# Hash attention and FFN on one core: whole-tile loads in one queue, part of the first batch's hash by column-tiled matmuls and moves, and a new order

## The chip, the core and the metric

The kernel runs on one core of a Trainium2 chip. The core has five engines that each work through their own list of instructions in order: TensorE (PE, the matrix unit; PEld is its loading of weights), VectorE (DVE), ScalarE (ACT), GpSimd (POOL) and SyncE (SP). Sixteen DMA engines move data between device memory (HBM) and the on-chip memory SBUF, or within SBUF; a transfer is started by an instruction on SP, ACT or POOL. Transfers issued by SP are on queue 1 of the trace, those issued by POOL on queue 0. Matmul results go to a second memory, PSUM. Engines wait for one another by semaphores, and a transfer reports its end by a semaphore too.

The metric is the time of one execution on the device in microseconds (us), as the median of several executions. Lower is better.

## The reference

Four batches of eight heads, 768 positions, 64 numbers each. Queries and keys are hashed by the signs of six projections, a query attends only to keys with the same hash, and the result goes through a normalization and a two-layer network (FFN) with a residual. In short:

```python
q_bits = (np.einsum('bhsd,dk->bhsk', q, proj) > 0)        # proj: 64 x 6
k_bits = (np.einsum('bhsd,dk->bhsk', k, proj) > 0)
mask = q_bucket[:, :, :, None] == k_bucket[:, :, None, :]  # bucket: the six bits as a number
scores = np.where(mask, scale * np.matmul(q, k^T), -1e9)
attn = softmax(scores)
x = np.matmul(attn, v)                                     # heads side by side: 768 x 512
xn = (x - mu) / np.sqrt(var + 1e-06) * g_ln
out = x + np.maximum(xn @ w_ch1, 0.0) @ w_ch2              # 512 -> 2048 -> 512
```

## The kernel before

**Tiling.** Work is cut into 12 units of 256 queries: unit u belongs to batch u // 3. The eight heads are two groups g of four, and the 768 keys are three pieces kp of 256. That makes 72 score tiles, numbered s = 6u + 3g + kp. Each tile is a list of small steps, written as words such as `S.t.7.2`: the step's name, the engine's letter (v DVE, a ACT, p POOL, s SP, t PE), and its arguments.

- `S` (function `S_`): scores of one tile by 24 matmuls. The mask is not a select: hash bits are stored in a tile `G` as +0.5 and -0.5, a matmul of the bits of keys and queries is added into the same PSUM as the scaled scores, and only equal hashes come out large enough to survive the exponential. The last argument is 2 for all four heads, or 0 or 1 for a half (the PSUM tiles scA and scB).
- `E`: the exponential on ACT, two instructions per tile, into a tile that has three buffers. `A`: attention times values, 16 matmuls into the PSUM tile `acc`.
- `na`, `nb`, `nc`, `ce`, `rs`: division by the row sum, statistics, and the normalized `xc`. `ft` and `fc` (unit 0 only) or `fl` (a DMA transpose) turn it into `xnT`.
- `F`: 8 matmuls of the first FFN layer; `R`: its relu, on DVE or ACT; `D`: 4 matmuls of the second layer; `Z`: residual; `O`: the store. From unit 1 on, all `F` use the one PSUM tile `f1`, so an `F` can start only when the `R` of the one before has read it.

**Loading and hashing.** Keys and queries come as 768 KB tiles `X` (one per batch, group, and q or k); DVE turns them (`tn` in batch 0, `tu` later) and ACT, DVE or POOL cast them to bf16 (`ca`, `CA`) as `qb` and `kb`. There are four buffers for `X`.

- Batch 0 is loaded in parts, `lx.s.g.t.from.to` (t is 0 for q and 1 for k; the last two are the pieces of 256 positions). Its hash is `ha`, two matmuls of 256 columns in f32 with the padded projection `pfull`, which leaves the bits of all four heads on the partitions where `S` wants them; `bi` on DVE makes them 0.5 or -0.5 and writes `G`. There are twelve `ha` and `bi`, one per group, q or k, and piece.
- Later batches are loaded whole (`LX.s.b.g.t`). Their hash is `hm`: 16 column-tiled matmuls with the small projection `p32`, which put the bits of different positions on different partitions; `bt` makes them 0.5 or -0.5 in a tile `B`, and 16 small transfers per group, `mo`, bring them to their places in `G`.
- v comes as `lv`: two whole transfers of 768 KB for batch 0, and transfers of 192 KB for the others. POOL casts it (`cv`), sets a column of ones (`on`) and sums it (`su`); `sp` on PE and `sc` spread the sum. The weights come as eight transfers issued by POOL, `lw1` and `lw2`, which turn f32 into bf16 on the way.

**What sets the order.** Nothing is scheduled while the kernel is built. The string `ORDER` lists some 1,100 words; the loop at the end reads them one by one, and each engine's instructions follow in that order. What the layer below adds is the waits: for data, for a free buffer, and for the transfers. There are eight completion semaphores for the transfers of SP and ACT, which take them in turn, so that a transfer is issued only when the one eight before it has landed (where no other wait implies it).

The functions `hq`, `bq` and `mq` are in the kernel before too, but no word of its `ORDER` calls them.

Of the kernel before, what the change touches and what calls it, by code (L numbers as in the profile page):

```python
# [17 lines left out]
lp.a mem.v tab.a lx.s.0.0.0.1 warm.t tn.v.0.0.0 pf.v ha.t.0.0.0 lx.s.0.1.1.3 ca.a.0.0.0 tn.v.0.1.2 ha.t.0.1.2  # L18
tn.v.0.1.1 bi.v.0.0.0 ha.t.0.1.1 lx.s.0.1.0.1 tn.v.0.1.0 ca.a.0.1.0 bi.v.0.1.2 ca.p.0.1.2 S.t.2.0 E.a.2.0 S.t.2.1
E.a.2.1 lv.s.1.0.0 on.p.0 on.p.1 lx.s.1.0.0.1 ha.t.0.1.0 bi.v.0.1.1 lw1.p.3 ca.v.0.1.1 S.t.1.0 E.a.1.0 S.t.1.1  # L20
E.a.1.1 tn.v.1.0.0 ca.v.1.0.0 bi.v.0.1.0 ha.t.1.0.0 S.t.0.0 bi.v.1.0.0 E.a.0.0 S.t.0.1 E.a.0.1 pmem.p p32.p
lv.s.0.0.4 cv.p.0.0.0 cv.p.0.0.2 su.p.0.0 lx.s.1.1.0.3 tn.v.1.1.1 ha.t.1.1.1 ca.v.1.1.1 bi.v.1.1.1 A.t.1.1
lv.s.1.0.3 A.t.1.0 lw1.p.0 lv.s.1.0.2 S.t.4.2 E.a.4.1 E.a.4.0 tn.v.1.1.0 ha.t.1.1.0 bi.v.1.1.0 ca.p.1.1.0 A.t.0.1
A.t.2.1 tn.v.1.1.2 ca.p.1.1.2 sp.t.0.0 sc.v.0.0 A.t.0.0 A.t.2.0 na.v.0.0 nb.v.0.0 nc.v.0.0 S.t.3.2 E.a.3.1 E.a.3.0
ha.t.1.1.2 bi.v.1.1.2 S.t.5.2 E.a.5.0 E.a.5.1 lx.s.0.0.1.3 tn.v.0.0.1 ha.t.0.0.1 tn.v.0.0.2 ca.v.0.0.1 lv.s.0.4.4
cv.p.0.4.2 cv.p.0.4.0 A.t.3.2 A.t.4.2 su.p.0.4 sp.t.0.4 lg.s sc.a.0.4 bi.v.0.0.1 S.t.8.2 E.a.8.1 lx.s.1.0.1.3
tn.v.1.0.1 ca.p.1.0.1 tn.v.1.0.2 ca.v.1.0.2 ha.t.1.0.2 ha.t.1.0.1 bi.v.1.0.2 lw1.p.2 LX.s.1.0.0 tu.v.1.0.0.1
tu.v.1.0.0.3 E.a.8.0 S.t.7.2 E.a.7.0 E.a.7.1 A.t.5.2 LX.s.1.0.1 tu.v.1.0.1.3 bi.v.1.0.1 LX.s.1.1.0 ha.t.0.0.2
S.t.6.2 E.a.6.0 E.a.6.1 na.v.0.1 A.t.8.2 A.t.7.2 nb.v.0.1 nc.v.0.1 ce.v.0.0 ce.v.0.1 ft.t.0.1 fc.a.0.1 lw1.p.1
ca.p.0.0.2 bi.v.0.0.2 lv.s.1.4.3 lw2.p.0 ft.t.0.0 S.t.9.2 E.a.9.1 E.a.9.0 lv.s.1.0.1 su.p.1.0 cv.p.1.0.0  # L30
tu.v.1.0.1.1 fc.v.0.0 F.t.0.7 R.v.0.7 F.t.0.6 R.a.0.6 lv.s.1.4.2 LX.s.2.0.0 lw2.p.2 A.t.6.2 na.v.1.0 nb.v.1.0
nc.v.1.0 tu.v.1.0.1.0 S.t.10.2 E.a.10.0 E.a.10.1 lw2.p.1 F.t.0.0 R.v.0.0 A.t.9.2 F.t.0.5 R.a.0.5 S.t.11.2 E.a.11.1
E.a.11.0 rs.p.0 tu.v.1.0.0.2 tu.v.1.0.1.2 CA.p.1.0.1 LX.s.1.1.1 lv.s.1.4.0 A.t.10.2 F.t.0.2 R.v.0.2 lv.s.1.4.1
cv.p.1.4.0 F.t.0.1 R.v.0.1 S.t.14.2 E.a.14.0 E.a.14.1 A.t.11.2 F.t.0.4 R.a.0.4 tu.v.1.0.0.0 F.t.0.3 R.a.0.3 na.v.1.1
nb.v.1.1 nc.v.1.1 ce.v.1.1 fl.s.1.1 ce.v.1.0 fl.s.1.0 A.t.14.2 CA.v.1.0.0 S.t.12.2 E.a.12.1 hm.t.1.0 bt.v.1.0
mo.s.1.0.2.3 tu.v.1.1.0.3 tu.v.1.1.1.3 tu.v.1.1.0.1 tu.v.1.1.0.2 tu.v.1.1.1.1 mo.s.1.0.0.2 mo.s.1.0.0.3 mo.s.1.0.0.0
mo.s.1.0.3.2 mo.s.1.0.3.3 mo.s.1.0.1.1 tu.v.1.1.1.2 D.t.0.0.0 E.a.12.0 S.t.13.2 E.a.13.0 mo.s.1.0.2.2 mo.s.1.0.1.0
tu.v.1.1.0.0 mo.s.1.0.0.1 D.t.0.0.1 D.t.0.0.2 F.t.1.2 R.v.1.2 tu.v.1.1.1.0 E.a.13.1 S.t.16.2 E.a.16.1 E.a.16.0
F.t.1.1 R.v.1.1 A.t.12.2 A.t.13.2 F.t.1.0 R.v.1.0 S.t.15.2 E.a.15.1 mo.s.1.0.2.1 LX.s.2.0.1 F.t.1.5 R.v.1.5
mo.s.1.0.3.0 lw2.p.3 D.t.0.0.3 mo.s.1.0.3.1 E.a.15.0 mo.s.1.0.1.2 hm.t.1.1 S.t.17.2 E.a.17.0 E.a.17.1 mo.s.1.0.1.3  # L40
su.p.1.4 mo.s.1.0.2.0 na.v.2.0 A.t.16.2 nb.v.2.0 A.t.15.2 nc.v.2.0 bt.v.1.1 mo.s.1.1.1.0 mo.s.1.1.0.0 mo.s.1.1.0.3
# [547 lines left out]
```

## Time and profile before

| | |
|---|---|
| median of 3 executions | 312.07 us (311.89 to 312.83) |
| profiled execution | 312.83 us; its span 311.1 us |
| PE busy | 294.3 us, 95% of the span |
| DVE, ACT, POOL busy | 185.7, 181.5, 89.7 us |
| read from HBM, written to it | 27.53 MB, 6.29 MB |
| first score matmul | 10.36 us |
| first FFN matmul | 39.01 us |

The span is what the profile covers; what lies around it is the difference to the execution's time, 1.7 us. Times in the profile count from the start of the span. A line of the order of time reads: start, length, engine, source line, operation, output <- inputs, shape, number of instructions merged, and in brackets how long the engine was idle before and what ended that. PE's records overlap, since matmuls are pipelined and their ends are modelled. "Packet records" are the DMA engines' own list of what they moved and when.

### The profile page before, as it was taken

What the parts mean: (1) busy time and instruction counts of PE and PEld (TensorE: products, weight loads), DVE (VectorE), ACT (ScalarE), POOL (GpSimd) and SP (SyncE); (2) the same over time, 40 slices, a digit from 0 to 9 for tenths busy, and PEclk for the clock granted to TensorE, in tenths of its full rate; (3) what the DMA queues carried; (4) which work ended last, traced back from release to release, by engine and by line L of the source; (5) the groups of instructions that cost most, each with busy time, mean ns of one, the idle gap of its engine ahead of it and who ended that gap; (6) DMA issues with size and microseconds to landing.
All of it is one profiled execution on the core that took longest, in us unless ns stands there. A gap on an engine that the chain in (4) does not pass through costs nothing.

```text
span 311.1 us, 9787 instructions
## 1 busy us (share of the span) xinstructions
PE 294.3 (95%) x4296; PEld 206.5 (66%) x4336; DVE 185.7 (60%) x357; ACT 181.5 (58%) x197; POOL 89.7 (29%) x103
## 2 busy tenths in 40 slices
PE   7997799799999899989999999999999999999995
PEld 6675587576677557667667666667667676775663
DVE  3578868768442984978364668443544547246432
ACT  2666687454678655665456787655666777661000
POOL 0869570602403650416705304300300101001000
PEclk9999999999999999999999999999999999999999
DMA  7999999840299317511430901401300400502122
GB/s 177 286 301 361 238 208 261 91 125 9 42 244 300 128 24 179 166 38 35 100 79 2 204 8 30 87 11 33 94 2 2 103 0 13 93 2 60 43 70 68
DMA packets 30426, 33.58 MB, mean 108 GB/s; under 512 B 15536, under 2 KB 27056, under 8 KB 30384
## 3 DMA queue, kind: packets, MB, share of 16 engines
q1 hardware_dynamic: 25792, 28.50, 36.0%
q0 software_dynamic: 4224, 4.19, 8.3%
q8 instruction: 34, 0.56, 0.7%
q10 hardware_dynamic: 368, 0.26, 0.3%
q14 instruction: 8, 0.07, 0.1%
HBM read 27.53 MB, written 6.29 MB: 109 GB/s over the span
## 4 chain that ended last, share of the span: by engine, by line
PE 73%; DMA 14%; POOL 4%; DVE 4%; issue 3%; SPq 1%; DVEq 0%; POOLq 0%
PE f L510 25%; PE sc L438 13%; PE acc L453 8%; DMA vn<-in_v_dram 8%; DMA w_sb<-in_moe_w_ch_dram 5%; POOL t L369 2%; PE hp L403 1%; POOL vaug L361 1%; DMA xnT<-xc 1%; PE f_100None L526 1%; PE f L526 1%; PE f_81None L526 1%; PE f_50None L526 1%; PE f_60None L526 1%; PE f_90None L526 1%
## 5 line engine op out<-in xcount | busy, mean ns | idle before, releaser
L444 ACT ACTIVATE E<-sc,bias_sb 128x1024 bf16<-128x1024 f32 x144 | 152.7, 1110 | 72.3 <-PE sc L438 71.3
L510 PE MATMUL f<-xnT,w_sb 128*128 128x256 bf16 x768 | 99.3, 273 | 1.5 <-DVE B L246 1.2
L510 PEld LDWEIGHTS <-w_sb 128*128 128x128 bf16 x768 | 70.9, 98 | 23.6 <-issue 10.0
L520 DVE TENSOR_SCALAR hb<-f 128x512 bf16<-128x512 f32 x52 | 35.9, 690 | 58.9 <-PE f L510 58.3
L526 PEld LDWEIGHTS <-hb 128*128 128x128 bf16 x400 | 37.5, 98 | 36.0 <-issue 5.1
L438 PE MATMUL sc<-qb,kb 32*128 32x256 bf16 x1152 | 53.4, 267 | 0.0
L518 ACT ACTIVATE hb<-f 128x512 bf16<-128x512 f32 x44 | 26.1, 597 | 39.5 <-PE f L510 39.5
L453 PEld LDWEIGHTS <-E 128*128 128x128 bf16 x1152 | 41.1, 98 | 6.5 <-issue 4.3
L438 PE MATMUL sc<-G 6*128 6x256 bf16 x576 | 42.6, 273 | 2.4 <-DVE G L246 1.3
L453 PE MATMUL acc<-vaug,E 128*128 128x65 bf16 x1152 | 44.6, 194 | 0.0
L488 POOL TENSOR_SCALAR rs<-mv 128x2 f32<-128x2 f32 x12 | 7.1, 594 | 99.8 <-DVE mv L482 99.5
L438 PEld LDWEIGHTS <-kb 32*128 32x128 bf16 x1152 | 31.1, 93 | 1.6
L438 PEld LDWEIGHTS <-G 6*128 6x128 bf16 x576 | 15.6, 91 | 22.2 <-issue 18.2
L243 DVE STREAM_TRANSPOSE T<-X 128x384 f32<-128x384 f32 x48 | 24.9, 553 | 0.8 <-POOL kb L254 0.8
L369 POOL TENSOR_TENSOR t<-vn 128x768 f32<-128x768 f32 x8 | 14.6, 1819 | 33.4 <-DMA vn<-in_v_dram 33.3
L466 DVE SCALAR_TENSOR_TENSOR y<-vsB,acc 128x520 f32<-128x520 f32 x24 | 16.6, 691 | 10.9 <-PE acc L453 10.8
L483 DVE SCALAR_TENSOR_TENSOR xc<-x,mv,gB 128x512 bf16<-128x512 f32 x24 | 22.5, 938 | 0.8
L252 POOL TENSOR_SCALAR qb<-T 128x1536 bf16<-128x1536 f32 x3 | 12.7, 4243 | 28.4 <-DVE mv L482 15.5
L361 POOL CAST vaug<-vn 128x768 bf16<-128x768 f32 x16 | 13.5, 854 | 20.1 <-DMA vn<-in_v_dram 20.1
L475 DVE TENSOR_TENSOR x<-y,rc 128x512 f32<-128x512 f32 x24 | 18.7, 778 | 0.8
L479 DVE BATCH_NORM_STATS2 st<-x 128x6 f32<-128x256 f32 x48 | 18.0, 417 | 0.7
L312 PE MATMUL hf<-tp,pfull 128*128 128x256 f32 x48 | 14.9, 450 | 0.7 <-DVE pfull L277 0.7
(96 smaller groups left out, 229.6 us busy)
## 6 DMA issues: line engine op xcount, KB each, us to landing
out_dram<-res SPq DMA_DIRECT2D x44, 128.0 KB
X<-in_k_dram SPq DMA_DIRECT2D x7, 768.0 KB
vn<-in_v_dram SPq DMA_DIRECT2D x24, 192.0 KB
X<-in_q_dram SPq DMA_DIRECT2D x6, 768.0 KB
w_sb<-in_moe_w_ch_dram POOLq DMA_DIRECT2D x8, 512.0 KB, 12.5
vn<-in_v_dram SPq DMA_DIRECT2D x2, 768.0 KB
G<-B SPq DMA_DIRECT2D x96, 4.5 KB
X<-in_q_dram SPq DMA_DIRECT2D x2, 512.0 KB
```

The lines of the kernel that those rows point to most:

```text
L243: nc.vector.transpose(d[:, j], s[:, j, kj0 : kj0 + n])
L369: nc.gpsimd.tensor_tensor(t3, s[:, 0:3], s[:, 3:6], op=AOP.add)
L438: nc.tensor.matmul(sc(s, i // 2)[:, i % 2, 256 * kk : 256 * kk + 256], lh, rh, start=(rep == 0), stop=(rep == 2), skip_group_check=True,)
L444: nc.scalar.activation(E(s)[:, heads(h)], sc(s, h), AF.Exp, scale=EXP_SCALE, bias=bias_sb)
L453: nc.tensor.matmul(acc[:, qt, (D + 1) * i : (D + 1) * (i + 1)], E(s)[:, i, 256 * kk + P * qt : 256 * kk + P * qt + P], vaug(u // 3)[:, 4 * ...
L475: nc.vector.tensor_tensor(xo, a[:, :, :, 0:D], rc.to_broadcast([P, 2, 4, D]), op=AOP.mult)
L479: nc.vector.bn_stats(stats(u)[:, qt, g], xt(u)[:, qt, 256 * g : 256 * g + 256])
L483: nc.vector.scalar_tensor_tensor(xc(u)[:, t], xt(u)[:, t], mv(u)[:, t, 0:1], gB, op0=AOP.subtract, op1=AOP.mult,)
L510: nc.tensor.matmul(f1[:, n].rearrange("p (t x) -> p t x", t=2), w1_sb[:, dt, P * nt : P * nt + P], xnT(u)[:, :, dt], start=(dt == 0), stop ...
L518: nc.scalar.activation(hb(u)[:, 2 * p : 2 * p + 2], f1, AF.Relu)
L520: eng.tensor_scalar_max(hb(u)[:, 2 * p : 2 * p + 2], f1, 0.0)
L526: nc.tensor.matmul(f2, hb(u)[:, nt, P * t : P * t + P], w2_sb[:, nt, half(h)], start=(nt == 0), stop=(nt == NNT - 1),)
```

## The change

Only `ORDER` changes; the code is the same, and the line numbers behind the string grow by 2. The differences in the list of steps, apart from `R`, `sc`, `CA` and `O` words that change their engine (`R`: 44 on ACT and 52 on DVE become 36 and 60):

- The hash of the queries 256 to 767 of batch 0: the four `ha` and four `bi` for t = 0 and pieces 1 and 2 go. In their place stand two `hq` (one per group; 8 column-tiled matmuls of 128 columns each), two `bq` on DVE, and 32 transfers `mq` on SP of 6 partitions by 128 positions, which bring the bits to `G`:

```python
def hq(eng, g):
    hp = ps(f"hq{g}", [P, P], "f1")
    for j in range(2):
        for c in range(4):
            nc.tensor.matmul(
                hp[32 * c : 32 * c + 32], p32[:, j], tp(g, 0, 1 + c // 2)[:, j, P * (c % 2) : P * (c % 2) + P],
                start=(j == 0), stop=(j == 1), skip_group_check=True,
            )
def bq(eng, g):
    bits(Bq(g), made[f"hq{g}"])
def mq(eng, g, c, i):
    eng.dma_start(
        out=Gt(0, g)[32 * i : 32 * i + NB, 0, 256 + P * c : 256 + P * c + P],
        in_=Bq(g)[32 * c + 8 * i : 32 * c + 8 * i + NB],
    )
```

- Score tile 3 is done in two halves instead of whole.
- All else is order. The first loads are the first piece of k (256 KB) and the first of q, then the rest of k in one transfer; v of batch 1 (`lv.s.1.*`), of which three parts of 192 KB came early, now comes behind the moves; the weights come as `lw1` 1, 0, 3, 2 and `lw2` 1, 0, 2, 3 instead of `lw1` 3, 0, 2, 1 and `lw2` 0, 2, 1, 3. The word `tab`, an activation on one column, moves from the start to the middle. The units' steps are interleaved anew to the end.

The start of the string, cut:

```diff
-lp.a mem.v tab.a lx.s.0.0.0.1 warm.t tn.v.0.0.0 pf.v ha.t.0.0.0 lx.s.0.1.1.3 ca.a.0.0.0 tn.v.0.1.2 ha.t.0.1.2
-tn.v.0.1.1 bi.v.0.0.0 ha.t.0.1.1 lx.s.0.1.0.1 tn.v.0.1.0 ca.a.0.1.0 bi.v.0.1.2 ca.p.0.1.2 S.t.2.0 E.a.2.0 S.t.2.1
...
-S.t.6.2 E.a.6.0 E.a.6.1 na.v.0.1 A.t.8.2 A.t.7.2 nb.v.0.1 nc.v.0.1 ce.v.0.0 ce.v.0.1 ft.t.0.1 fc.a.0.1 lw1.p.1
-ca.p.0.0.2 bi.v.0.0.2 lv.s.1.4.3 lw2.p.0 ft.t.0.0 S.t.9.2 E.a.9.1 E.a.9.0 lv.s.1.0.1 su.p.1.0 cv.p.1.0.0
-tu.v.1.0.1.1 fc.v.0.0 F.t.0.7 R.v.0.7 F.t.0.6 R.a.0.6 lv.s.1.4.2 LX.s.2.0.0 lw2.p.2 A.t.6.2 na.v.1.0 nb.v.1.0
...
+mem.v lx.s.0.1.0.1 tn.v.0.1.0 warm.t pmem.p lp.a pf.v p32.p ca.a.0.1.0 lx.s.0.0.0.1 tn.v.0.0.0 ca.a.0.0.0 ha.t.0.1.0
+bi.v.0.1.0 ha.t.0.0.0 bi.v.0.0.0 S.t.0.0 E.a.0.0 S.t.0.1 E.a.0.1 lx.s.0.1.1.3 tn.v.0.1.1 tn.v.0.1.2 ca.p.0.1.2
+ha.t.0.1.1 ca.p.0.1.1 ha.t.0.1.2 bi.v.0.1.1 S.t.1.1 E.a.1.1 bi.v.0.1.2 S.t.2.0 E.a.2.0 lx.s.1.1.0.3 tn.v.1.1.1
+ca.v.1.1.1 tn.v.1.1.0 ha.t.1.1.1 bi.v.1.1.1 S.t.2.1 lv.s.0.0.4 cv.p.0.0.0 S.t.1.0 lx.s.1.0.0.1 tn.v.1.0.0 ha.t.1.0.0
+ca.v.1.0.0 E.a.1.0 cv.p.0.0.2 lx.s.0.0.1.3 tn.v.0.0.1 tn.v.0.0.2 ha.t.1.1.0 bi.v.1.1.0 on.p.0 A.t.0.0 lw1.p.1 lg.s
+A.t.0.1 lx.s.1.0.1.3 lv.s.0.4.4 LX.s.1.0.0 bi.v.1.0.0 ca.v.0.0.1 hq.t.0 LX.s.1.0.1 lw1.p.0 E.a.2.1 S.t.4.2 A.t.2.1
+E.a.4.1 E.a.4.0 A.t.2.0 bq.v.0 mq.s.0.0.3 mq.s.0.0.2 mq.s.0.0.0 mq.s.0.1.1 mq.s.0.1.3 mq.s.0.1.2 mq.s.0.0.1
+mq.s.0.1.0 tn.v.1.1.2 ha.t.1.1.2 ca.v.1.1.2 su.p.0.0 lw1.p.3 ca.p.1.1.0 S.t.3.1 S.t.3.0 E.a.3.1 A.t.1.0 tu.v.1.0.0.0
+cv.p.0.4.0 bi.v.1.1.2 sp.t.0.0 mq.s.0.2.3 mq.s.0.2.2 mq.s.0.3.2 A.t.1.1 tn.v.1.0.2 ca.v.1.0.2 E.a.3.0 S.t.5.2
+E.a.5.1 mq.s.0.2.0 lw1.p.2 E.a.5.0 cv.p.0.4.2 tn.v.1.0.1 sc.v.0.0 na.v.0.0 A.t.3.1 A.t.4.2 nb.v.0.0 hq.t.1 lw2.p.1
+S.t.7.2 E.a.7.1 tu.v.1.0.1.0 mq.s.0.3.1 nc.v.0.0 bq.v.1 mq.s.1.1.2 mq.s.1.3.3 mq.s.1.1.1 mq.s.1.3.1 mq.s.1.0.3
+mq.s.1.3.0 mq.s.1.1.3 A.t.3.0 tu.v.1.0.1.2 mq.s.0.2.1 lw2.p.0 su.p.0.4 sp.t.0.4 A.t.5.2 ca.p.0.0.2 E.a.7.0 S.t.6.2
+E.a.6.0 E.a.6.1 sc.v.0.4 na.v.0.1 A.t.7.2 nb.v.0.1 nc.v.0.1 ce.v.0.0 ce.v.0.1 ft.t.0.0 ft.t.0.1 fc.a.0.1 rs.p.0
+S.t.8.2 E.a.8.1 E.a.8.0 fc.v.0.0 F.t.0.7 F.t.0.2 R.v.0.7 F.t.0.1 R.a.0.1 lw2.p.2 mq.s.0.3.0 mq.s.0.3.3 S.t.12.2
...
```

## The prediction

> **What bounds the kernel now.** I read the page's summary first, then the table of windows, TensorE's waits, and last the order of time around the start.
>
> ```profile
> PE 294.3 (95%) x4296; PEld 206.5 (66%) x4336; DVE 185.7 (60%) x357; ACT 181.5 (58%) x197; POOL 89.7 (29%) x103
> ...
> PE   7997799799999899989999999999999999999995
> ...
> DMA  7999999840299317511430901401300400502122
> ```
>
> TensorE is busy 95% of the span, so the time is its work plus its gaps. The last row says that the DMA engines are full in the first 50 us: there the data sets the pace.
>
> ```profile
> 20.00:25.00 5.00, 3.67 (x78) 2.76 (x80) 4.54 (x12) 3.46 (x4) 2.88 (x4) 1.00 1.13 313
> 25.00:30.00 5.00, 4.08 (x80) 3.08 (x73) 4.13 (x10) 2.92 (x4) 4.49 (x4) 1.00 1.07 376
> 30.00:35.00 5.00, 4.17 (x61) 2.97 (x63) 3.75 (x9) 3.81 (x4) 4.02 (x5) 1.00 1.05 274
> 35.00:40.00 5.00, 4.11 (x95) 3.28 (x87) 3.70 (x9) 3.48 (x4) 2.59 (x2) 1.00 1.12 241
> ```
>
> Second figure: PE busy; the last three: granted clock, DMA share, GB/s. The gaps are at the start: 20 to 40 us lack 4.0 us. Later TensorE waits little:
>
> ```profile
> PE f_00None L526 <- DMA w_sb<-in_moe_w_ch_dram: 1.6, 1, 1.6
> ...
> PE f L510 <- DVE B L246: 1.2, 1, 1.2
> ...
> PE vp L376 <- DVE B L246: 1.0, 1, 1.0
> ```
>
> 1.65 us at 56.9 us for the second weight matrix, 0.99 at 107.6, 1.21 at 133.0. The rows that price the change:
>
> ```profile
> 14.17 1.13 PE L312 MATMUL hf<-tp,pfull 128*128 128x256 f32 x4
> ...
> 39.01 1.92 PE L510 MATMUL f<-xnT,w_sb 128*128 128x256 bf16 x16
> ...
> 52.03 1.51 PE L403 MATMUL hp<-T,p 128*32 128x192 f32 x32
> ```
> ```profile
> 17.42 0.63 SPq L389 DMA_DIRECT2D X<-in_q_dram  x1
> 21.35 0.33 SPq L389 DMA_DIRECT2D X<-in_k_dram  x1
> ...
> 56.41 8.68 SPq L415 DMA_DIRECT2D G<-B  x11
> ```
>
> One hash of 256 positions (ha) holds PE for 1.13 us; a hash of a later batch (hm) takes 1.51; the first FFN matmul (F) starts at 39.01; a move of hash bits costs SP 8.68/11 = 0.79 us to issue.
>
> **TensorE's work falls by 3.5 us.** Four ha go: 4 x 1.13 = 4.5. Two hq come. Each has 8 matmuls of 128 columns against hm's 16 of 192: 1.44 (hm's common duration) x 1024/3072 = 0.5 each. Four bi of 0.42 us on DVE give way to two bq, as small. DVE is 60% busy; I count nothing.
>
> **An earlier start that buys nothing.** The first two loads are now 256 KB each and the first score tile needs only them, so it can start near 8.4 us (transposes from 4.04, 0.77 us each; pf 0.65; two ha; a bi of 0.42) against 10.36. That lead is lost at the next point, where PE must wait anyway, so I count 0. ScalarE's table is still loaded in front of its first activation, so moving tab costs its 0.20 us, hidden.
>
> **The new wait: score tile 7 behind eight moves.** Tile 7 (S.t.7.2) holds queries 256 to 511 of group 0 and is the first to read moved bits. It needs all eight moves mq.s.0.0.* and mq.s.0.1.*. They stand on SP behind the loads LX.1.0.0 and LX.1.0.1, 768 KB each, and every SP transfer waits in the built program for the transfer eight before it, whose completion semaphore it takes over. So the eighth move waits until LX.1.0.1 has landed. When is that?
> - Before, the trace's packet records end this load at 30.2 us, with 576 KB of batch 1's v ahead of it that now come later (three pieces, 0.55 us each when alone: 1.7) and two weight loads (2.55 us each when alone, from the run of four at 40.8 to 48.5). Both gone: 23.4. Both there: 28.5.
> - The first two weight loads follow on's memsets on GpSimd: v lands about 12.5, two casts of 0.85, the memsets 0.6, so issue at 14.8. Before, 8.76 to the first packet at 13.92 is 5.2 us, so they start near 20. The 3.4 us that the load then lacks go at half rate, as rows side by side did from 22 to 29 us: 20 + 6.8 = 27, between the ends.
> - The move is then issued at 27.3. Before, the move issued at 56.41 had its packets at 58.3 to 58.4: 1.9 us. The third of that row was due at 59.9 and came at 62.1, 2.2 us late, beside one weight load (packets 59.8 to 63.4). In the new kernel six weight loads keep queue 0 full from 20 to about 39, so I take the late row: 27.3 + 1.9 + 2.2, and 0.2 for the semaphore, is 31.6. Bounds: 23.4 + 0.3 + 1.9 + 0.2 = 25.8 and 28.5 + 0.3 + 4.3 = 33.1.
>
> [...] The trace shows four moves held back and then landing together, so I keep 2.2.
>
> **From tile 7 to the first F: 7.8 us.** PE does tile 7 (0.77), half of A.3 (0.25 to 0.35), sp (0.28), A.5 (0.65); A.5 ends 2.1 us after the start. Then unit 0's norm on DVE: 0.70 + 0.20 + 0.69 + 0.75 + 2 x (0.20 + 0.75) = 4.3 with small gaps 4.5; the second transposes end at 7.0 and tile 8 stands ahead of F (0.8). So F starts at 31.6 + 7.8 = 39.4, against 39.01. By then before has done 10 score tiles and 8 attention tiles (A), the new kernel 9 and 7: 0.77 + 0.49 of PE work more is still to come. The four spared ha are already inside this comparison, since all hashing is done by F in both. Lag at F: 0.4 + 0.77 + 0.49 = 1.7.
>
> **Behind F.** Tile 12 needs fifteen more moves: SP issues them in 15 x 0.79 = 11.9 us from about 28.2, so the last lands at 40.1 + 1.9 = 42.0, or 44.2 under weights. PE wants tile 12 three F later, at 42.2. I take 0.3 (0 to 2.0). The 32 moves hold SP for 32 x 0.79 = 25 us in all, between about 19 and 59. That delays LX.1.1.0 from 25.9-29 to about 40 and LX.1.1.1 to 45, and batch 1's v to 45 to 54; their readers (hm.1.1, sp.1.0) come near 60 us, hence 0, and only if these waited over 10 us more would PE notice. On GpSimd the first half of the second weight matrix is now issued at 24 to 26, some 25 us ahead of its first reader: the 1.65 us wait at 56.9 goes. The sum su.0.4 stands behind those two issues (1.6) and takes 1.82 + 0.85 + 0.81 = 3.5, to about 29.4, and sp needs it at 32: hidden.
>
> **The remade rest.** From unit 1 on, F has one PSUM bank: the next F waits for the relu of the last (0.69, with about 0.3 of hand-over: 1.0 us). Summing the PE work (S 0.77, A 0.49, F 0.87, D 0.84, hm 1.44) that each order puts between two F, the shortfall below 1.0 is 2.2 us in 21 places before and 3.6 us in 27 places after, the worst between F.1.3 and F.1.1. I take 1.2 (0 to 1.4). The two later waits for DVE (0.99 and 1.21) belong to the old order; the new one has the same kinds of places, so I take as much again, with -2.2 and +2.2 as ends. The last 6 us keep their form: 0.
>
> **Sum.** +1.7 - 1.65 + 0.3 + 1.2 = +1.6 us. The profiled execution took 312.83 (span 311.1 and 1.7 around it), the highest of three; the median is 0.8 lower. So 314.4 against the profiled execution, and 313.7 against the median of 312.07.
>
> **Rivals.**
> - SP's queue passes the weights (faster): queue 0 does not slow queue 1. LX.1.0.1 then lands at 23.4 to 25, the move 2.4 us behind it, and tile 7 starts at 25.8 to 27.4 (PE's own order allows about 26, after tile 5 near 25). The lag shrinks by 4.2 to 5.8 us: 307.9 to 309.5. It decides from a start below 29.0, where 2.6 us are gained and 311.1 is reached. For it: before, this load's own packets took only 1.9 us (28.3 to 30.2) though a weight load ran beside it until 29.4. Against it: the four moves held back at 60 us.
> - The moves starve until the weight queue is empty (much slower). Six loads of 2.55 from 20, with 3.4 of X between, end at 38.7; tile 7 then starts at 39 to 40, and the time is 321 or 322. Against it: the even sharing of large packets. For it: moves waited for nearly all of the one weight load that met them.
> - The start is a draw and the two later waits have no successor: 313.7 - 2.2 = 311.5, no change. For it: TensorE's work is 3.5 us less, and both waits come from one DVE queue whose order is all new.
>
> **How the numbers follow.** A measurement of this kernel can tell about 0.3%, 0.9 us, from no change. Forecast: 0.52, with times from 312.2 (tile 7 at 30.1) to 315.9 (tile 7 at 33.1 and 0.7 more at tile 12). Moves pass: 0.20. Starve: 0.11. Draw: 0.17. Slower than 313.0 are 0.44 of the forecast's 0.52 and the starved case: 0.55. Faster than 311.1 are the first rival and 0.04 of the draw: 0.24. The rest, 0.21, is no change. The range leaves out the starved case and the lowest end of the first: 309.5 to 317.5.
>
> **What would show it.** Score tile 7 starting near 31.6 us right after a DMA wait on G, with PE idle before it for several microseconds; ha at 8 times 1.13 and hq near 0.5; no wait for w_sb at the first D; the first F at 39 to 40. The prediction is wrong if tile 7 starts before 29 or after 35, or if a wait that I gave nothing (X or v of batch 1, or DVE's queue around 100 to 135 us) exceeds 2 us.

## The result, and the profile after

The new kernel takes 327.22 us in the median of 4 executions (325.11 to 328.63); the old one, run beside it on the same chip, 312.45. The ratio is 1.0473, with a 95% interval of 1.0398 to 1.0549: slower by 4.7%. The prediction said slower, with 313.7 and a range up to 317.5; the loss is about ten times what it summed up. The profiled execution took 325.11, 12.3 more than the old kernel's.

The page's summary of the new kernel: busy time of each engine, TensorE and its granted clock in 40 slices, and the chain that ended last.

```profile
PE 298.8 (92%) x4307; PEld 209.7 (65%) x4352; DVE 196.8 (61%) x366; ACT 176.2 (55%) x187; POOL 90.9 (28%) x102
...
PE   7976899889989989799999999999999999999995
...
PEclk9998559999999999999999999999999999999999
...
PE 63%; DVE 18%; SPq 7%; POOL 4%; DMA 4%; issue 3%; DVEq 0%; POOLq 0%
```

Two things are new. The chain runs through VectorE for 18% of the span, where it was 4%; and the fifth and sixth slices have TensorE at half its clock. The table of windows shows the same stretch (behind the window and its length come the busy times of PE, PEld, DVE, ACT and POOL with their instructions, then granted clock, DMA share and GB/s):

```profile
15.00:20.00 5.00, 4.59 (x51) 3.29 (x49) 4.83 (x8) 3.56 (x4) 4.92 (x7) 1.00 1.07 367
20.00:25.00 5.00, 3.29 (x67) 2.35 (x70) 4.97 (x10) 2.12 (x2) 4.92 (x7) 1.00 1.21 248
25.00:30.00 5.00, 2.54 (x65) 1.87 (x59) 4.85 (x10) 3.34 (x4) 4.83 (x6) 1.00 1.17 253
30.00:35.00 5.00, 4.37 (x70) 3.40 (x71) 3.37 (x8) 1.04 (x2) 1.65 (x2) 0.50 1.25 206
35.00:40.00 5.00, 3.96 (x65) 3.12 (x63) 3.75 (x10) 3.39 (x4) 0.00 (x0) 0.50 0.60 99
40.00:45.00 5.00, 4.70 (x43) 2.99 (x43) 1.41 (x3) 3.36 (x4) 3.11 (x4) 0.50 0.53 161
```

From 15 to 30 us VectorE is busy 14.65 of 15.00 and GpSimd 14.67, while TensorE falls to 2.54 of 5. The old kernel's VectorE had 4.54 and 4.13 of 5 in the windows from 20 and 25. Then the granted clock is 0.50, and a PE that looks busy does less: eight score matmuls take 0.64 us at 42.17, at half clock, and 0.39 at 47.69, at full clock. In the order of time, VectorE's row of that stretch reads:

```profile
16.75 2.72 DVE L254 TENSOR_SCALAR qb<-tp 128x512 bf16<-128x512 f32 x1
19.40 1.41 DVE L245 STREAM_TRANSPOSE tp<-X 128x256 f32<-128x256 f32 x4
...
21.38 1.65 DVE L254 TENSOR_SCALAR qb<-tp 128x512 bf16<-128x512 f32 x1
22.95 0.27 DVE L248 TENSOR_SCALAR Bq<-hq 128x128 bf16<-128x128 f32 x1
...
23.93 2.30 DVE L256 CAST kb<-tp 128x512 bf16<-128x512 f32 x1
...
27.73 1.04 DVE L254 TENSOR_SCALAR qb<-tp 128x512 bf16<-128x512 f32 x1
...
29.88 0.70 DVE L468 SCALAR_TENSOR_TENSOR y<-vsB,acc 128x520 f32<-128x520 f32 x1
```

and GpSimd's, beside the first of these casts:

```profile
17.34 1.84 POOL L371 TENSOR_TENSOR t<-vn 128x768 f32<-128x768 f32 x1
```

The first cast ends just after GpSimd's addition does. The transposes between the casts keep their length: four in 1.41 us, as at 9.85 us with GpSimd idle. The four casts of queries and keys in this stretch take 7.71 us together (2.72, 1.65, 2.30, 1.04). The first and the last lie beside an addition on GpSimd, the two between them beside its casts and its issuing of weight loads:

```profile
20.81 0.79 POOL L347 DMA_DIRECT2D w_sb<-in_moe_w_ch_dram  x1
21.59 1.07 POOL L256 CAST kb<-tp 128x512 bf16<-128x512 f32 x1
22.60 1.10 POOL L363 CAST vaug<-vn 128x768 bf16<-128x768 f32 x1
23.65 0.74 POOL L347 DMA_DIRECT2D w_sb<-in_moe_w_ch_dram  x1
24.39 0.84 POOL L363 CAST vaug<-vn 128x768 bf16<-128x768 f32 x1
25.16 1.48 POOL L350 DMA_DIRECT2D w_sb<-in_moe_w_ch_dram  x2
26.65 1.83 POOL L371 TENSOR_TENSOR t<-vn 128x768 f32<-128x768 f32 x1
```

The old kernel's trace had the same thing on a small scale, in a place where nobody waited for it: of two equal casts there, one lies beside an addition on GpSimd, the other beside one of GpSimd's own casts. VectorE's and GpSimd's order of time of the old kernel:

```profile
25.79 1.16 DVE L252 TENSOR_SCALAR qb<-tp 128x512 bf16<-128x512 f32 x1
...
29.29 0.43 DVE L252 TENSOR_SCALAR qb<-tp 128x512 bf16<-128x512 f32 x1
```
```profile
24.86 1.81 POOL L369 TENSOR_TENSOR t<-vn 128x768 f32<-128x768 f32 x1
```

What follows from it, in TensorE's and SyncE's order of time:

```profile
21.17 0.64 PE L326 MATMUL hq<-tp,p 128*32 128x128 f32 x16 [1.43 <-DVE G L248]
...
30.63 1.50 PE L455 MATMUL acc<-vaug,E 128*128 128x65 bf16 x24 [1.93 <-DVE y L468]
...
33.14 0.55 PE L440 MATMUL sc<-G 6*128 6x256 bf16 x4
...
42.75 4.89 PE L512 MATMUL f<-xnT,w_sb 128*128 128x256 bf16 x24
```
```profile
23.25 17.55 SPq L338 DMA_DIRECT2D G<-Bq  x23
```

TensorE waits for VectorE ahead of hq and ahead of A.3; tile 7 starts at 33.14 (forecast 31.6), the first F at 42.75 (forecast 39.4), and its 24 matmuls take 4.89 us, where `e7` below took 2.87 for them at full clock. SyncE's row of moves is as forecast. Later, TensorE's waits are these:

```profile
PE f L512 <- DVE hb L522: 2.0, 2, 1.7
...
PE f L512 <- DVE B L248: 1.8, 1, 1.8
PE hq L326 <- DVE G L248: 1.4, 1, 1.4
PE vp L378 <- POOL vsum L373: 1.3, 1, 1.3
```

The old kernel's wait of 1.65 for w_sb has gone, as forecast. The waits of 0.3 us or more behind 55 us sum to 7.6 (57.85, 71.9, 93.4, 118.7, 134.6 and 186.3 us), against 3.85 before.

The old kernel's own executions spread from 310.5 to about 316, with now and then one of 317 to 330, and the runs were made on several chips, so experiments are read by their ratio to the old kernel on the same chip, in which executions more than 1.5% above the fastest of their kernel are left out, and differences under about 2 us between two experiments are not taken as shown.

### The profile page after: what moved, and what is told of

The parts are those of the page before. It is cut to its first block, busy times and chain, and to the rows that moved or that the text cites. A ratio compares the mean times of both kernels' runs of the same rounds, so it can differ in the third digit from the quotient of the medians.

```text
span 323.1 us, 9848 instructions
## 1 busy us (share of the span) xinstructions
PE 298.8 (92%) x4307; PEld 209.7 (65%) x4352; DVE 196.8 (61%) x366; ACT 176.2 (55%) x187; POOL 90.9 (28%) x102
## 4 chain that ended last, share of the span: by engine, by line
PE 63%; DVE 18%; SPq 7%; POOL 4%; DMA 4%; issue 3%; DVEq 0%; POOLq 0%
PE f L512 21%; PE sc L440 10%; PE acc L455 8%; SPq L417 3%; DVE x L477 3%; SPq L338 2%; DVE qb L254 2%; DVE xc L485 2%; DVE T L245 2%; DVE tp L245 2%; POOL qb L254 2%; PE hf L314 2%; DVE y L468 1%; DMA G<-Bq 1%; PE hp L405 1%
## 5 line engine op out<-in xcount | busy, mean ns | idle before, releaser
L512 PE MATMUL f<-xnT,w_sb 128*128 128x256 bf16 x768 | 101.3, 277 | 5.0 <-DVE hb L522 2.0
L522 DVE TENSOR_SCALAR hb<-f 128x512 bf16<-128x512 f32 x60 | 41.3, 689 | 65.7 <-PE f L512 65.4
L440 PE MATMUL sc<-qb,kb 32*128 32x256 bf16 x1152 | 55.3, 273 | 0.2 <-POOL kb L256 0.2
L455 PEld LDWEIGHTS <-E 128*128 128x128 bf16 x1152 | 43.5, 99 | 10.4 <-issue 5.0
L455 PE MATMUL acc<-vaug,E 128*128 128x65 bf16 x1152 | 47.1, 196 | 1.9 <-DVE y L468 1.9
L520 ACT ACTIVATE hb<-f 128x512 bf16<-128x512 f32 x36 | 21.5, 596 | 31.7 <-PE f L512 31.7
L363 POOL CAST vaug<-vn 128x768 bf16<-128x768 f32 x16 | 15.6, 980 | 57.6 <-DMA vn<-in_v_dram 41.5
L485 DVE SCALAR_TENSOR_TENSOR xc<-x,mv,gB 128x512 bf16<-128x512 f32 x24 | 20.7, 863 | 0.9
L477 DVE TENSOR_TENSOR x<-y,rc 128x512 f32<-128x512 f32 x24 | 20.7, 863 | 0.8
L254 POOL TENSOR_SCALAR qb<-T 128x1536 bf16<-128x1536 f32 x3 | 12.3, 4100 | 11.8 <-DVE T L245 11.8
L314 PE MATMUL hf<-tp,pfull 128*128 128x256 f32 x32 | 10.0, 460 | 1.5 <-DVE pfull L279 1.0
```

What stands on the lines that cost most here:

```text
L254: eng.tensor_scalar(dst, src, QS, None, op0=AOP.mult)
L440: nc.tensor.matmul(sc(s, i // 2)[:, i % 2, 256 * kk : 256 * kk + 256], lh, rh, start=(rep == 0), stop=(rep == 2), skip_group_check=True,)
L455: nc.tensor.matmul(acc[:, qt, (D + 1) * i : (D + 1) * (i + 1)], E(s)[:, i, 256 * kk + P * qt : 256 * kk + P * qt + P], vaug(u // 3)[:, 4 * ...
L477: nc.vector.tensor_tensor(xo, a[:, :, :, 0:D], rc.to_broadcast([P, 2, 4, D]), op=AOP.mult)
L485: nc.vector.scalar_tensor_tensor(xc(u)[:, t], xt(u)[:, t], mv(u)[:, t, 0:1], gB, op0=AOP.subtract, op1=AOP.mult,)
L512: nc.tensor.matmul(f1[:, n].rearrange("p (t x) -> p t x", t=2), w1_sb[:, dt, P * nt : P * nt + P], xnT(u)[:, :, dt], start=(dt == 0), stop ...
```

## Where the loss is made: two hybrids

The order was cut at the first F. `e5` takes the new order up to there and the old order's words, in their order, for what is left; `e6` the reverse.

```diff
 e5: new words up to F.t.0.1 R.a.0.1 R.v.0.2, the 9 moves still due, then the old words not yet done
 e6: old words up to R.a.0.6 ... E.a.10.1 lw2.p.1, A.t.9.2 A.t.10.2, then the new words not yet done (no mq)
```

> The new kernel's order up to its first three F, then the old kernel's order for everything that is left (the nine moves still due stand directly behind the head). Counting TensorE's nominal work in the two traces, the new kernel is some 7.5 us behind the old one at 50 to 80 us and some 12 us behind from 200 us on. Theory 'the loss is made in the first 50 us': 312.8 + 7.5 = 320 us, 318.5 to 322. Rival 'most of the loss is made by the waits of the new order from 55 us on': 316 us or less.

> The mirror of the run before it: the old kernel's order up to its first two F (all batch-0 hashing as the old kernel does it, no moves of the new kind; A.9 and A.10 placed at the seam), then the new kernel's order for what is left. Theory 'first 50 us': only the waits of the new tail are paid, 12 - 7.5 = 4.5 us: 317 us, 315.5 to 318.5. Rival 'the new tail': 321 us or more. If both this and the run before come out near 312, the loss needs both parts together.

Measured: `e5` 322.33 us, ratio 1.0273 (1.0197 to 1.0349). `e6` 320.19, 1.0195 (1.0108 to 1.0282). Both times lie somewhat above what was expected, short of the rival's 321 for `e6`. Both parts lose, and 2.7% and 2.0% add up to the 4.7% of the whole.

The same can be read without medians. Each unit and group has one RECIPROCAL on VectorE (in `nb`), 24 in a run, which serve as milestones where two orders agree:

| start of the reciprocal, difference in us | u1 g0 | u2 g0 | u3 g0 | u5 g0 | u8 g0 | u11 g1 | end of span |
|---|---|---|---|---|---|---|---|
| `e5` less old (same tail) | +8.7 | +10.3 | +10.3 | +9.6 | +9.6 | +9.2 | +9.2 |
| new less `e6` (same tail) | +17.6 | +7.3 | +8.6 | +8.7 | +8.3 | +6.9 | +6.9 |

Once the start is over, the lag stays: 7 to 10 us are lost before the second unit is through and little is added by an equal tail. (u1 g0 in the second row lies at the seam and can't be compared.) By the spans the new tail costs 323.1 - 320.3 = 2.8 us behind the new head and 316.2 - 311.1 = 5.1 behind the old one, where some 1.7 of waits stand at the seam itself. So the start costs 7 to 9 us and the order behind it 3 to 5.

## The start: casts beside GpSimd

Three runs bear on VectorE's late casts. In `e2` four of them go to ScalarE; in `e12` also the GpSimd cast `ca.p.0.0.2` goes ahead of the sums; in `e8` the casts stay and GpSimd's two sums of v are replaced by a constant, so that this part of the computation is missing.

```diff
 e2, e12:
-ca.v.1.0.0 ca.v.0.0.1 ca.v.1.1.2 ca.v.1.0.2
+ca.a.1.0.0 ca.a.0.0.1 ca.a.1.1.2 ca.a.1.0.2
 e12 besides:
-su.p.0.0 ... su.p.0.4 sp.t.0.4 A.t.5.2 ca.p.0.0.2
+ca.p.0.0.2 su.p.0.0 ... su.p.0.4 sp.t.0.4 A.t.5.2
 e8, in su:
+        if b == 0:
+            nc.gpsimd.memset(vsum(b)[:, D * hs : D * (hs + 4)], 1.0)
+            return
```

> The changed kernel with four casts of batch 0 moved from VectorE to ScalarE (ca.1.0.0, ca.0.0.1, ca.1.1.2, ca.1.0.2). Theory VectorE: these four took 2.72, 1.65, 2.30 and 1.04 us beside GpSimd's work instead of 0.43 to 0.63, which made everything behind them late by 5.8 us; ScalarE takes them in 0.6 to 1.1 us each while it waits anyway. Then bq is done near 19.5 instead of 23.2, score tile 7 starts at 29 to 31 instead of 33.1, TensorE has no gap of 2 us ahead of it, the clock stays at 1.0, and the time is 316 to 320. Rival moves: the eighth move lands at 32.9 whatever VectorE does, as it waits for LX.1.0.1 and the weights; the gap only changes its place, the clock still falls, and the time is 324 to 328.

> The new kernel without batch 0's sums of v on GpSimd (two times three additions, 3.4 us each; a constant is written in their place, so this part of the computation is left out). Theory 'VectorE's casts are stretched by the GpSimd work beside them': the cast at 16.75 us, 2.72 us long, falls to 0.43; bq follows at 20.7 or before, against 22.95; the attention tile A.3.1, which waited for the norm, starts at 29 or before, against 30.63, and the clock's fall at 30.3 may go with it: 323 us (320.5 to 325). Rival 'the casts wait for something else': 2.7 us as before and 326 to 328 us.

> The whole computation again: the new kernel with the four stretched casts on ScalarE, as in the run that moved them, and with the GpSimd cast ca.p.0.0.2 placed ahead of the first sums of v, so that the transpose tn.1.0.1 needn't wait for it (5.77 us in that run). Theory 'VectorE's lateness is most of what can be won back in the start': the first norm at 27 or before (30.9 in the new kernel), tile 7 at 31 by its moves, 323 us (321 to 324.5). Rival 'ScalarE's exponentials are late then, and take it': 325 us or more.

`e8` took 322.77 us, ratio 1.0284 (1.0206 to 1.0362), below the new kernel's interval. Its order of time on VectorE:

```profile
16.65 0.85 DVE L254 TENSOR_SCALAR qb<-tp 128x512 bf16<-128x512 f32 x1
...
19.86 0.73 DVE L254 TENSOR_SCALAR qb<-tp 128x512 bf16<-128x512 f32 x1
...
21.50 1.30 DVE L256 CAST kb<-tp 128x512 bf16<-128x512 f32 x1
...
24.30 0.43 DVE L254 TENSOR_SCALAR qb<-tp 128x512 bf16<-128x512 f32 x1
...
26.41 0.70 DVE L471 SCALAR_TENSOR_TENSOR y<-vsB,acc 128x520 f32<-128x520 f32 x1
```

The same four casts take 3.31 us and not 7.71, and the norm (y) starts 3.5 us earlier, at 26.41 against 29.88. The theory's mechanism is shown: without GpSimd's additions the casts are shorter, and 4.4 us of the run go. (GpSimd's other work moved up too, so the additions' own 3.4 us each are part of it.) What is not separated is how much each kind of GpSimd's work stretches a cast: three of the four in `e8` still take more than 0.43, and no addition lies beside them. A cast took 0.43 at the shortest here, at 24.30, and 2.72 beside an addition in the new kernel; by what mechanism GpSimd's work lengthens it, no run shows.

The first F in `e8` starts at 39.39, the forecast's 39.4, and the run is still some 9 us above the old kernel. So the late casts were not all.

`e2` took 325.48, 1.0344 (1.0252 to 1.0436), a miss of its theory. `e12`'s four executions ran from 321.65 to 327.48 (ratio 1.0307, 1.0181 to 1.0433, from the lower two, 321.65 and 325.14), and with the theory at 321 to 324.5 they decide nothing. In `e2` bq came at 20.28 and not 22.95, but the transpose tn.1.0.1 then got a tile that GpSimd still had to read and waited 5.77 us for `ca.p.0.0.2`. With that cast ahead, in `e12`, another GpSimd cast was late, `ca.p.1.1.0`. Its waits:

```profile
PE sc L438 <- POOL kb L254: 4.0, 2, 3.2
PE sc L438 <- ACT E L444: 2.3, 2, 1.2
PE sc L438 <- DMA G<-Bq: 2.3, 1, 2.3
```

In `e2`, where GpSimd is busy 14.68 of 15.00 us from 15 to 30, taking work from VectorE moved the wait to what GpSimd does next. In the profile of `e12`, its fastest execution, there is such a wait too, but the norm (y) starts at 27.89 and the first F at 40.90, some 2 us earlier each than in the new kernel; what this repair is worth stays open.

## The start: the halved clock

The trace's record of the granted clock says when it changed: it was at half in the new kernel from 30.01 to 47.08. Was that a loss by itself? The fillers are matmuls into a free PSUM tile, placed where TensorE waits anyway; `e1` has two, `e7` six, `e9` five in the kernel without the sums.

```diff
+    def wm(eng, n, k, bank=0):
+        wp = ps(f"wm{k}", [P, P], ("f2", "scA")[bank])
+        for _ in range(n):
+            nc.tensor.matmul(wp, ones, ones, start=True, stop=True)
 e1: wm.t.12.0 before sp.t.0.0, wm.t.34.1 before A.t.3.1
 e7: wm.t.24 before hq.t.0, 10 before ha.t.1.1.2, 14 before sp.t.0.0, 34 before A.t.3.1, 22 before S.t.6.2, 16 before ft.t.0.0
 e9: e8, and 12 before S.t.5.2, 8 before A.t.3.1, 20 before S.t.7.2, 24 before S.t.6.2, 10 before ft.t.0.0
```

> The changed kernel with 46 matmuls of ones by ones added (12 ahead of sp.t.0.0, 34 ahead of A.t.3.1) into a PSUM tile that nobody reads, so that TensorE is not idle at 26 to 27 us and 28.6 to 30.6 us. Theory clock: the granted clock fell to half from 30.2 to 47.2 us because TensorE had been nearly idle from 26 to 30.6, and this costs 4 to 8 us: the clock stays at 1.0 from 20 to 50 us, score tile 12 starts near 44 instead of 47.6, and the time falls from 327 to 319 to 323. Theory data: moves and VectorE set the pace up to tile 12 and the slow clock only fills their waits: the clock stays up, but the time falls by less than 2 us.

> The new kernel with filler matmuls in six places of the first 40 us where TensorE waits (24, 10, 14, 34, 22 and 16 of 128 columns, 0.054 us each), so that no stretch of 3.4 us is less than about 0.7 busy. They use free time only, so the data is as late as it was. Theory 'the half clock from 30.3 to 47.4 us costs by itself': the first F starts at 41.5 or before and its 24 matmuls take 2.8 us and not 4.89; the run ends 4 us earlier, 323 us (321.5 to 324.5) against 327.2. Rival 'TensorE would have waited for data anyway': 325.5 or more, with the clock at 1.0 and the waits longer.

> The kernel without batch 0's v sums (that part is again left out) with fillers in the five places between 25 and 37 us where TensorE still waited in it (12, 8, 20, 24, 10 matmuls). In that run the first F started at 39.39, within 0.4 us of the old kernel, yet its 24 matmuls took 4.60 us because the clock was at half from 33.2 to 43.5. Theory 'now that the data is in time, the half clock costs': F takes 2.8 us, the following stage moves up by 2 to 3 us, 320 us (318.5 to 321.5) against 322.8. Rival 'the next wait takes it': 322 or more, the clock nearly 1.0 all the same.

`e1`: 325.0 us, 1.0326 (1.0244 to 1.0408); that is 2.2 us below the new kernel by the medians and 4.6 by the ratios, whose intervals overlap. The clock fell twice in the start all the same, at 22.1 and 39.1, where other gaps were left. `e7`: 326.84, 1.0403 (1.0313 to 1.0492), at half clock for 6.8 us and not 17.1; F took 2.87 us and not 4.89, and the run gained 0.4 us by the medians and 2.2 by the ratios, which is within the spread, though a transpose of this run also waited 2.92 us for GpSimd, which it didn't in the new kernel. `e9`: 321.48, 1.0252 (1.0157 to 1.0346), with the clock full until 51.4 in its profile: 1.3 us less than `e8`, within the spread. So the half clock was no large part of the loss, and the rival has the better of it: much of what the clock gives back, the next wait takes. In `e9` this is the moves, 3.5 us of waits on `G<-Bq`. A gain of a microsecond or two is not ruled out.

To see the clock by itself, `e4` puts three gaps into the old kernel: a row of small VectorE memsets, the last of which a matmul waits for.

```diff
+    def gp(eng, n, k):
+        wp = ps(f"gp{k}", [P, P], "f2")
+        for _ in range(n):
+            nc.vector.memset(jf, 0.0)
+        nc.vector.memset(jb, 1.0)
+        nc.tensor.matmul(wp, jb, ones, start=True, stop=True)
 gp.t.14.0 after Z.v.4.1, gp.t.26.1 after Z.v.6.1, gp.t.46.2 after Z.v.8.1
```

> The kernel before with three gaps made in TensorE's work, by a matmul that waits for a row of 14, 26 or 46 memsets on VectorE (behind Z.v.4.1, Z.v.6.1, Z.v.8.1, about 165, 210 and 260 us), each about 0.06 to 0.1 us. It adds the gaps and leaves out nothing. Theory clock: the granted clock goes to 0.5 after a gap and stays there for 5 to 17 us of full work; the question is from which length on. By the gaps of the two kernels (1.2 us without a fall, 1.9 us behind two shorter ones with a fall) I expect no fall at the first (about 1 us), perhaps one at the second (about 2) and one at the third (about 4). If no gap lowers the clock, the fall in the changed kernel has another cause.

One execution: 338.7 us. The gaps came out at 1.91, 5.85 and 9.7 us, and the windows around the first two show the clock behind each (third figure from the right):

```profile
170.00:175.00 5.00, 3.21 (x39) 1.80 (x37) 2.36 (x17) 3.43 (x5) 3.93 (x4) 1.00 0.37 93
175.00:180.00 5.00, 4.83 (x25) 2.38 (x29) 4.00 (x10) 0.48 (x2) 1.45 (x2) 0.66 0.63 189
...
220.00:225.00 5.00, 1.65 (x7) 0.57 (x6) 2.27 (x15) 2.04 (x2) 0.00 (x0) 0.88 0.49 119
225.00:230.00 5.00, 2.49 (x22) 2.00 (x23) 1.50 (x14) 0.46 (x1) 0.00 (x0) 0.50 0.07 18
```

Even the gap of 1.91 us brought 3.4 us at half clock, where the old kernel's single waits of 1.65 at 56.9 and 1.21 at 133.0 did not (granted clock 1.00 in its windows from 55 to 60 and 130 to 135). The execution is 25.3 us above the median of the old kernel beside it (313.39), of which the gaps are 17.5; some 8 are left, beside 23.9 us at half clock in all (3.4 of it ahead of the first gap). That is an estimate from a single execution, but it says that where TensorE has work to do, the half clock does cost time.

## The start: the moved hash bits

`e3` undoes the hash part alone in the new order; `e14` does so in `e8`; `e13` in `e10`, the kernel of the next section, with fillers and two late waits mended.

```diff
-hq.t.0   bq.v.0   hq.t.1   bq.v.1   and all mq.s.*
+ha.t.0.0.1 ha.t.0.0.2   bi.v.0.0.1 bi.v.0.0.2   ha.t.1.0.2 ha.t.1.0.1   bi.v.1.0.2 bi.v.1.0.1
```

> The changed kernel with the hash of the old one: four ha and four bi in the places of the two hq and bq, no moves mq. Everything else in the new order. Rival moves: without them tile 7 waits for nothing on the DMA side and the time goes back to 312 to 316. Theory VectorE and order: TensorE gets 4.5 us of ha in place of 1 us of hq, which fills the gap and holds the clock, but VectorE's stretched casts, the new order's later waits (1.7 at 57.8, and some 5 us more between 70 and 200) stay: 317 to 321.

> The same question without fillers and without the two mended waits: the new kernel without batch 0's v sums (left out again; 322.8 us with the moves) and with ha and bi in place of hq, bq and the moves. With the sums in, undoing the moves changed nothing (327.7 against 327.2). Theory 'next bound': 320.5 us or less. Rival: 322 to 325, that is, the moves cost no more than the 3.5 us of TensorE that they spare.

> The kernel of the run with fillers, without batch 0's v sums and with the two late waits mended (319.6 us), but with batch 0's later queries hashed as in the old kernel: ha and bi in place of hq, bq and the 32 moves. TensorE's work rises by 3.5 us, partly in time in which it waits. In that kernel tile 7 and a tile at 47.7 us wait for moves (1.7 to 3.5 us in two profiles) and the row of moves holds SyncE from 19.4 to 37.5 us ahead of the next batch's loads. Theory 'behind the late casts the moves are the next bound': 317.5 us or less. Rival 'the moves are paid by what they spare TensorE': 319 to 322.

`e3`: 327.73 us, 1.0443 (1.0362 to 1.0523), no change; its cast at 16.71 takes the same 2.72, and its tn.1.0.1 waited 2.91 for GpSimd, which hides up to that much of a gain. `e14`: 322.49, 1.0300 (1.0194 to 1.0406), no change against `e8`. `e13`: 316.97, 1.0139 (1.0042 to 1.0237), all four executions (316.3 to 317.47) below `e10`'s lowest of 318.14. That is 2.6 us by the medians, on two chips, and 1.5 by the ratios, whose intervals overlap, so the size is not shown. So the moves are not what made the kernel slow; they become a bound only when the casts, the clock and two later waits are out of the way. In `e10` a wait on them had appeared:

```profile
PE sc L447 <- DMA G<-Bq: 1.7, 1, 1.7
```

## Behind the start

Two of the new order's late waits were mended: the cast of group 0's queries of batch 1 on VectorE as in the old order, where GpSimd takes 4.08 us and VectorE's transposes wait 2.45 for it, and `sp.t.1.4` four matmuls further back.

```diff
 e10: e9, and
-CA.p.1.0.0      sp.t.1.4 D.t.1.0.3 Z.v.1.0
+CA.v.1.0.0      D.t.1.0.3 sp.t.1.4 Z.v.1.0
```

> The run before it with two edits behind 50 us: the cast of group 0's queries of batch 1 on VectorE and not on GpSimd, where it took 4.08 us and VectorE's transposes waited 2.45 for it, and the product with the sums of v (sp.t.1.4) placed behind D.1.0.3. Theory 'two of the new order's late waits, 1.73 at 57.85 and 1.31 at 93.4, are the price of GpSimd's order': both go, less 0.5 that stays, 2 to 2.5 us less than the run before it. Rival 'VectorE is as late then': within 0.7 of it.

`e10`: 319.59 us, 1.0186 (1.0109 to 1.0263), 1.9 less than `e9`, just short of the expected 2 to 2.5 and within the spread. `e18` below shows more: its edit, the same one in `e14`, took 322.49 to 317.31, 5.2 us by the medians on two chips and 3.2 by the ratios; the highest execution of the one lies just below the lowest of the other (319.21 and 319.30).

Four runs then ask which repair does what. `e15` computes everything: batch 0's sums of v on TensorE, hash undone, the two waits mended, no fillers. `e17` is `e15` with `e9`'s fillers, `e18` is `e13` without them. `e16` is the old kernel with the sums on TensorE.

```diff
 e15, e16, e17, in sp (and no su for batch 0):
+        if b == 0:
+            for kj in range(KJ):
+                nc.tensor.matmul(vp, ones, vaug(b)[:, hs : hs + 4, kj, 0:D], start=(kj == 0), stop=(kj == KJ - 1))
```

> The whole computation: the new kernel's order with batch 0's sums of v made on TensorE (ones times the six slices of v, added up in PSUM: 12 matmuls of 256 columns, 0.11 us each, in place of two, and no additions on GpSimd), hash undone (ha, bi), and the two late waits mended; no fillers. Theory 'the loss is the casts beside GpSimd, then the moves, then the two waits': as the kernel with the same repairs and fillers, 317.0, plus 1.1 for the matmuls and less what the fillers cost: 315.5 to 319. Rival 'it was the fillers that did it, by the clock': 321 or more, with the clock at 0.98 or below.

> The old kernel with batch 0's sums of v on TensorE in the same way. There TensorE waits 0.92 us for the sum at 28.39 and the casts on VectorE beside GpSimd's additions take 1.16 where 0.43 is their own time; TensorE's work rises by 1.1 us. Theory 'GpSimd's sums cost the old kernel something too': 0.5 to 1.5 us less, a ratio of 0.995 to 0.998. Rival 'in the old order nobody waits for these casts': 1.000 to 1.004.

> The whole computation: the kernel with batch 0's sums on TensorE, hash undone and the two waits mended (321.6 us), with the five fillers (74 matmuls, 4 us if none of them finds free time) back in. Its sibling with fillers and without the sums took 317.0. Theory 'the fillers made that difference, by holding the clock': 318 us or less. Rival 'the difference was one wait of 2.74 us for the transposed rows at 68 us and the clock's fall behind it, which come and go': 320 to 323, with that wait there.

> The fourth corner: batch 0's sums left out, hash undone, the two waits mended, no fillers. With fillers it took 317.0 us and the clock was 0.998 or above in all runs. Theory 'the fillers hold the clock': 320 us or more, with the clock at 0.99 or below in some runs. Rival 'they do nothing': 316 to 318.

| | median us | ratio to the old kernel |
|---|---|---|
| `e13` no sums, fillers | 316.97 | 1.0139 (1.0042 to 1.0237) |
| `e18` no sums, no fillers | 317.31 | 1.0196 (1.0116 to 1.0275) |
| `e17` sums on TensorE, fillers | 319.10 (320.25 with one of 326.13) | 1.0264 (1.0182 to 1.0346) |
| `e15` sums on TensorE, no fillers | 321.59 | 1.0320 (1.0248 to 1.0391) |
| `e16` old order, sums on TensorE | 312.32 | 0.9994 (0.9956 to 1.0032) |

The fillers make 0.3 us (`e18` to `e13`) and 2.5 (`e15` to `e17`) by the medians, 1.8 and 1.7 by the ratios. With `e7` and `e9` that is four pairs, all of one sign and none clear of the spread: the clock's part of the loss is some 0 to 2.5 us. In `e15`, which leaves nothing out, the four casts of the start take 3.17 us (0.96, 0.42, 1.36, 0.43), as short as in `e8`. Sums on TensorE cost 2 to 4 us more than no sums, though 12 matmuls of 0.11 are 1.3 (in `e15` two rows of six, 0.83 each); why is open (the profile of `e15` has one wait of 2.74 us for the transposed rows at 68 us, but that came and went in other kernels too). In the old order the sums can go to TensorE or stay on GpSimd, 0.9994, which fits casts beside them that nobody there waits for. So the sums as such cost the old order nothing; what costs is that the new order puts the casts beside them.

`e11` tried one word in the old kernel, the last waits of the first D in mind: quarter 1 of the second weight matrix ahead of quarter 2 (`lw2.p.1 ... lw2.p.2` in place of `lw2.p.2 ... lw2.p.1`).

> The old kernel with one change: the load of quarter 1 of the second weight matrix ahead of quarter 2. In the old kernel's trace the seventh weight load landed at 56.3 and the first D waited 1.65 us for it at 56.93. With quarter 1 as the sixth (landed at 48.5) D can go on at 55.3 with four matmuls of 0.24; then quarter 2 is waited for. 0.9 us less if nothing else moves: a ratio of 0.997. Rival: the queue lets the wait move to quarter 2 whole, 1.000.

Inconclusive: its six executions ran from 311.42 to 321.75, the old kernel's beside it from 311.62 to 325.18, and no ratio can be given. No version beat the old kernel.

## Why the prediction was right or wrong

**Direction right, size wrong.** Three of its steps held: the wait for w_sb went (-1.65); TensorE's hash work fell, hq taking 0.64 us at full clock where 0.5 was priced; the lead at the start bought nothing (first score at 9.99, forecast 8.4, and 10.36 before). By its packets LX.1.0.1 ended at 27.05, forecast 27, but that is partly luck: the load was issued only at 20.83, since its buffer was freed by transposes that stood on VectorE behind the cast of 2.72 (19.12 in `e8`, where it ended at 25.43), and the forecast had no such wait. The prediction's own packet times read 0.3 us late against the views of the trace (a move's first packets come 1.6 us after its issue and not 1.9), by which its 31.6 would have been some 31.0.

**The step that failed first: "DVE is 60% busy; I count nothing."** That is the mean over the span. In the windows that the prediction itself showed, the old VectorE had 4.54 and 4.13 of 5; the new order put a whole batch's transposes and casts there, beside GpSimd's additions, and VectorE became the bound of the start from 15 to 30 us. Casts moved to VectorE got no price, and the row of 1.16 beside 0.43 was not read; four of them took 7.71 us. Taking GpSimd's additions away gave 4.4 us back (`e8`).

**Tile 7.** Forecast 31.6, bounds 25.8 to 33.1; measured 33.14. The moves ran much as summed: they were issued from 23.25, when bq was done, about 0.75 apart, the eighth at 28.48 (forecast 27.3), and its packets had landed by 32.7. But TensorE was itself waiting for y until 30.63, and hq stood ahead of the tile until 33.1, so in the new kernel VectorE held the tile and not the moves, and the nearness of 33.14 to 31.6 is partly luck. With the moves undone the run was no faster (`e3` and `e14`), so tile 7's wait for moves, which the forecast was built on, did not set the end.

**"From tile 7 to the first F: 7.8 us".** Measured 9.6, all at half clock, which the prediction did not consider; but with the clock mostly full it still took 8.6 (`e7`, 35.15 to 43.78). And "0.77 + 0.49 of PE work more is still to come" was the term for the one tile not yet done at F. With an equal tail (`e5`) the lag grew from 3.2 us at F (42.24 against 39.01) to 9.5 at the first D (62.99 against 53.47): F at half clock, 4.29 us for 24 matmuls (about 1.5 more), waits of 0.84 and 1.65 for ScalarE's exponentials, 0.79 for moves, and the tile. 1.26 was priced, 6.3 came.

**"The remade rest. I take 1.2 (0 to 1.4)".** Between 2.8 and 5.1 by the hybrids. The two later waits for VectorE got successors of the same kind (0.90 at 71.9, 1.82 at 134.6, against 0.99 and 1.21), as assumed; what the term lacked are waits on GpSimd's order (1.73 at 57.85 behind a cast of 4.08 us, 1.31 at 93.4 for the sum of v) and on the transposes. Casts are not all that GpSimd stretches: the two waits of 0.90 and 1.82 stand behind the norm's multiply (x), 0.69 us at 30.84, which took 2.27 at 66.30 and 1.88 at 128.99, each beside an addition of 1.8 on GpSimd. But VectorE's instructions behind 50 us ran longer than the median of their kind by about as much in the old order (7.7 us in all, 8.4 in the new one), so it doesn't explain the tail by itself.

**Tile 12** was to wait 0.3 for moves; in the new kernel it didn't, since it started at 47.57 and not 42.2.

**The rivals.** "Moves pass" failed. "Starve" gave 321 or 322, near in size, by a mechanism that isn't there: tile 7 at 39 was its mark. No rival had VectorE as the bound of the start.

**What stays open.** With all repairs some 4 to 6 us remain (`e13`, `e18`); part may be the new order's other waits for VectorE and the transposes, the rest was not found. The single causes overlap, so their prices do not add up.

## What to carry to other kernels

Read an engine's share in the stage that the change fills, not over the span: 60% in the mean was over 85% where the work went. Price a VectorE cast by what GpSimd does beside it (0.42 to 2.84 us in these runs), and when a new order is made, look first for two engines that are both full in one stretch. And before a slow clock is blamed, ask what TensorE would have waited for at full speed.

## What the runs showed of the hardware

- Casts on VectorE from SBUF to SBUF (128x512, f32 to bf16) took 0.42 us at the least (`e15`, at 19.15) and up to 2.72 in the new kernel and 2.84 in `e7`, each beside a GpSimd addition of 1.84; the norm's multiply of two f32 inputs took 0.69 and up to 2.27 beside an addition of 1.82. A row of four transposes beside GpSimd's work took 1.41 in the new kernel, as long as with GpSimd idle, but 1.56 in `e15` and 1.67 in `e8`.
- The granted clock was at half for 17.07 us in the new kernel (30.01 to 47.08), twice for 6.8 in the start of `e1` (22.06 to 28.88 and 39.12 to 45.96), and for 3.4, 6.9 and 10.2 at the three gaps of `e4`. All of these are near multiples of 3.41. In pieces of that length, the new kernel's TensorE was busy for 0.40 of the one that ends with the fall at 30.01, for 0.82, 0.87, 0.82 and 0.91 of the next four and all of the fifth, behind which the clock was full again. The busy share alone does not tell when it falls: in the new kernel a piece of 0.47, from 132.41, passed at full clock, and in `e1` the clock fell at 22.06 behind one of at least 0.50. The longest single wait at the new kernel's fall was 1.93 us, from 28.70 to 30.63.
- At half clock for 17.1 us the new kernel should have lost some 6 to 7.5 us of matmul work (an estimate from TensorE's 15.11 us busy there: the lower end by F's 4.89 us against 2.87 in `e7`, the upper by half). Holding most of that off gained 0.4 us by the medians and 2.2 by the ratios (`e7`, 6.8 us left at half clock), and 1.3 and 1.0 in the kernel without the sums (`e9` against `e8`, 3.4 us left of 17.1), none of it clear of the spread: in much of that time TensorE would have waited anyway.
